# A third score area for the first batch's attention, with two PSUM banks merged into one tile

## The chip, the cores and the metric

The kernel runs on one core of one Trainium2 chip. The metric is the device time of a whole execution in microseconds (us), on a warm chip; spans and single instructions are read from a profiled execution, whose span is some 2 us shorter than the time (308.67 against 306.5 for the profiled run of the kernel before). "Faster" and "slower" mean a difference over 2% (6.2 us); medians are given with their range, and profiles decide where the time went.

## The reference, cut to what matters

```python
batch, n_heads, seq, head_dim = (4, 8, 768, 64); n_clusters = 16
n_tokens, d_model, d_ff = (3072, 512, 2048)

q_assign = argmax(einsum('bhsd,hcd->bhsc', q_n, c_n), axis=-1)   # k_assign likewise
mask = q_assign[:, :, :, None] == k_assign[:, :, None, :]
scores = where(mask, scale * q @ k.T, -1e9)
x = softmax(scores) @ v                     # (B*S, H*D) after a transpose
h = x @ w_in
g = h + sin(alpha * h)**2 / (alpha + 1e-9)
out = g @ w_out
```

Each head's queries and keys are assigned to one of 16 centroids, and only pairs with the same centroid attend. The kernel appends the one-hot assignment to q and k as 16 more rows of the contraction, so the mask costs no pass of its own.

## The kernel before

Four batches, one after the other: attention (48 "steps" a batch, each one key block of one head: two score matmuls, one exp of 128x768, six matmuls of probabilities by values), then the MoE layer (16 pieces). A step also carries preparations of later head pairs: transposes of q and k on TensorE, copies to SBUF on VectorE, casts to bf16 on GpSimd, the assignment matmuls and VectorE's one-hot.

PSUM has eight banks of 512 fp32. Two score areas take four, OB (output of attention) one, and three single banks M0, M1, M2 take the preparations in turn:

```python
SA = [psum.tile([P, 1024], F32, name=f"S{i}") for i in range(2)]
OB = psum.tile([P, 512], F32, name="OB")
M0 = psum.tile([P, 512], F32, name="M0")
M1 = psum.tile([P, 512], F32, name="M1")
M2 = psum.tile([P, 512], F32, name="M2")
# ...
banks = [M1, M2, M0]; held = set(); turn = [0]
def bank():                        # the next bank by turns that is not held
    while True:
        i = turn[0] % 3; turn[0] += 1
        if i not in held:
            return banks[i]

def area(i):                       # scores of step i
    return SA[(i // ASTEPS + i) % 2]

def prep_T(m, g, bk=None, eng="dve"):   # one of four: q or k, head 0 or 1 of pair m
    # three fp32 transposes into a bank, then one copy (VectorE or ScalarE) to SBUF
def prep_cast(m, h):               # GpSimd: two casts of 64x768 to bf16, 0.85 us each
def prep_v(m):                     # GpSimd: cast of the pair's v, 0.83 us
def load_qk(m, eng=nc.gpsimd):     # GpSimd issues two DMAs, 0.72 us each

class Fill:   # during attention of batches 1 to 3: output matmuls of the batch before,
              # accumulating in M1 or M0, which is held until its 16 are done
```

In MoE the third hidden area is the pair of banks (M1, M2), read in two pieces of 512 and 256. In the prologue `prep_T(0, 0, M1, "act")`, `prep_T(0, 1, M2, "act")` and later `prep_T(1, 0, M2, "act")`, `prep_T(1, 2, M1)` use both banks in turn.

The softmax here doesn't subtract the row's maximum and nothing guards it: scores larger than these inputs give would overflow.

## Time and profile before

| | before |
|---|---|
| time, median (range) | 308.21 us (308.18 to 308.46) |
| profiled span | 306.5 us |
| first exp starts | 11.93 us |
| batch 0: exps 0 to 12, exps 12 to 47 | 10.19, 26.56 us |
| attention of batches 1, 2, 3 (first exp to last) | 39.69, 38.73, 37.64 us |
| last exp to the next batch's first | 30.66, 31.38, 31.84 us |
| exps 80 to 81, exps 136 to 137 | 1.44, 1.05 us |

The rows add up to the span but for the tail after the last exp. They come from the start times of the 192 exps in the trace, which mark every step on the one engine that each step needs exactly once. The prediction shows the lines of the profile.

### The profile page before, as it was taken

The numbers are of one execution on the slowest core, as the hardware profiler recorded it, in microseconds if no ns is written. First come the engines' busy times: TensorE is split into PE (matmuls) and PEld (weight loads), VectorE is DVE, ScalarE is ACT, GpSimd is POOL, SyncE is SP. The second block draws the span as 40 slices with busy tenths as digits, with TensorE's granted clock in tenths as the row PEclk, the third lists the DMA queues.
The fourth block names the chain that finished last, engine by engine and source line by source line (L and its number), as shares of the span: only waits on it lengthen the run. The fifth ranks groups of instructions, "written<-read, shape, count | busy, mean of one in ns | idle before, by whom it ended". The sixth has DMA issues, their size and how long they took to land.

```text
span 306.5 us, 7197 instructions
## 1 busy us (share of the span) xinstructions
PE 300.6 (98%) x2727; PEld 177.9 (58%) x2727; DVE 206.6 (67%) x368; ACT 238.3 (78%) x323; POOL 140.4 (46%) x232
## 2 busy tenths in 40 slices
PE   8899999999999999999999999999999999999996
PEld 4466776555555666555456656555556666555543
DVE  3796666999867983688897485677865313667821
ACT  5689997976598988877589989687679999687300
POOL 6779988048364399983005189970001090000000
PEclk9999999999999999999999999999999999999999
DMA  7558999989668576971044577420012021000032
GB/s 215 166 165 237 309 261 234 215 182 325 127 178 195 122 154 156 305 295 51 2 120 108 108 182 161 119 86 2 0 72 60 33 47 46 29 7 2 0 127 78
DMA packets 31105, 40.48 MB, mean 132 GB/s; under 512 B 5904, under 2 KB 24928, under 8 KB 31072
## 3 DMA queue, kind: packets, MB, share of 16 engines
q0 software_dynamic: 10272, 21.12, 26.4%
q1 hardware_dynamic: 20560, 18.86, 23.7%
q8 instruction: 21, 0.34, 0.5%
q14 instruction: 12, 0.10, 0.1%
q10 hardware_dynamic: 240, 0.06, 0.1%
HBM read 27.30 MB, written 6.29 MB: 110 GB/s over the span
## 4 chain that ended last, share of the span: by engine, by line
PE 86%; ACT 10%; DVE 1%; issue 1%; DMA 1%; SPq 0%; ACTq 0%; DVEq 0%
PE M L406 19%; PE S L437 18%; PE S L338 11%; ACT pT L344 10%; PE OB L353 9%; PE M L437 8%; PE S L339 5%; PE OB L406 5%; PE M L222 3%; PE S L406 2%; PE M L144 2%; PE S L512 1%; DVE gT L462 1%; DMA QK<-ohT 1%; PE OB L377 1%
## 5 line engine op out<-in xcount | busy, mean ns | idle before, releaser
L344 ACT ACTIVATE pT<-S 128x768 bf16<-128x768 f32 x192 | 142.2, 810 | 14.8 <-PE S L339 13.7
L406 PE MATMUL M<-w_out_bf,gT 128*128 128x512 bf16 (+1 forms) x288 | 90.4, 376 | 0.0
L338 PE MATMUL S<-QK 80*128 80x512 bf16 x192 | 72.9, 380 | 1.4 <-ACT pT L344 0.6
L437 PEld LDWEIGHTS <-w_in_bf 128*128 128x128 bf16 x512 | 49.2, 98 | 38.0 <-issue 2.1
L353 PEld LDWEIGHTS <-pT 128*128 128x128 bf16 x1152 | 56.1, 97 | 21.2 <-ACT pT L344 0.2
L437 PE MATMUL S<-xT,w_in_bf 128*128 128x512 bf16 x352 | 66.1, 326 | 0.2 <-DVE gT L462 0.2
L353 PE MATMUL OB<-VX,pT 128*128 128x65 bf16 x1152 | 61.3, 193 | 0.0
L199 POOL TENSOR_SCALAR QK<-T 64x384 bf16<-64x384 f32 x80 | 42.8, 535 | 39.4 <-DMA T<-Tq 29.0
L450 ACT ACTIVATE s_sb<-S,alpha_col 128x768 bf16<-128x768 f32 (+2 forms) x45 | 39.7, 885 | 23.6 <-PE S L437 15.9
L406 PEld LDWEIGHTS <-gT 128*128 128x128 bf16 x400 | 38.4, 97 | 28.0 <-issue 1.2
L462 DVE SCALAR_TENSOR_TENSOR gT<-u_sb,ralpha,S 128x768 bf16<-128x768 bf16 (+2 forms) x45 | 44.6, 993 | 10.8 <-ACT u_sb L455 8.0
L339 PE MATMUL S<-QK 80*128 80x256 bf16 x192 | 51.9, 270 | 0.0
L399 POOL DMA_DIRECT2D xT<-xq x48 | 25.9, 547 | 23.2 <-DVE xq L391 22.2
L364 DVE RECIPROCAL rec<-OB 128x6 f32<-128x6 f32 x32 | 6.2, 195 | 36.6 <-PE OB L353 36.5
L437 PE MATMUL M<-xT,w_in_bf 128*128 128x512 bf16 (+1 forms) x160 | 30.6, 326 | 0.0
L339 PEld LDWEIGHTS <-QK 80*128 80x128 bf16 x192 | 18.8, 98 | 17.2 <-issue 2.2
L458 DVE TENSOR_TENSOR u_sb<-s_sb 128x768 bf16<-128x768 bf16 (+2 forms) x41 | 24.1, 589 | 6.1 <-ACT s_sb L450 6.1
L211 POOL CAST VX<-v 128x768 bf16<-128x768 f32 x16 | 13.3, 830 | 29.1 <-issue 28.1
L450 ACT ACTIVATE s_sb<-M,alpha_col 128x512 bf16<-128x512 f32 (+1 forms) x40 | 20.9, 574 | 6.9 <-PE M L437 6.8
L462 DVE SCALAR_TENSOR_TENSOR gT<-u_sb,ralpha,M 128x512 bf16<-128x512 bf16 (+1 forms) x40 | 22.8, 611 | 4.2 <-ACT u_sb L455 3.7
L406 PE MATMUL OB<-w_out_bf,gT 128*128 128x512 bf16 (+1 forms) x80 | 25.3, 347 | 0.0
L338 PEld LDWEIGHTS <-QK 80*128 80x128 bf16 x192 | 18.6, 97 | 8.4 <-issue 4.4
(86 smaller groups left out, 277.3 us busy)
## 6 DMA issues: line engine op xcount, KB each, us to landing
T<-Tq SPq DMA_DIRECT2D x80, 96.0 KB, 3.1
out_dram<-o_sb SPq DMA_DIRECT2D x23, 256.0 KB, 2.1
v<-in_v_dram POOLq DMA_DIRECT2D x14, 384.0 KB, 5.0
q<-in_q_dram POOLq DMA_DIRECT2D x13, 384.0 KB, 7.1
k<-in_k_dram POOLq DMA_DIRECT2D x13, 384.0 KB, 7.4
w_in_bf<-in_moe_w_in_dram POOLq DMA_DIRECT2D x4, 512.0 KB, 9.6
w_out_bf<-in_moe_w_out_dram POOLq DMA_DIRECT2D x4, 512.0 KB, 11.0
xT<-xq POOLq DMA_DIRECT2D x48, 24.0 KB, 2.3
```

The lines of the kernel that those rows point to most:

```text
L199: nc.gpsimd.tensor_scalar(out=QK[0:D, m % NQK, h, t].rearrange("c (n i a) -> c i n a", i=4, a=32)[:, 2 * par : 2 * par + 2], in0=src[:, t] ...
L211: nc.gpsimd.tensor_copy(out=VX[m % NVX][:, :, :, 0:D], in_=st[m]["v32"])
L338: nc.tensor.matmul(out=dst[:, 0:512], lhsT=lhsT, rhs=T[:, 0, 0:512], start=True, stop=True)
L339: nc.tensor.matmul(out=dst[:, 512:S], lhsT=lhsT, rhs=T[:, 0, 512:S], start=True, stop=True)
L344: nc.scalar.activation(out=pT, in_=area(i)[:, 0:S], func=ACTF.Exp, scale=escale)
L353: nc.tensor.matmul(out=o3[:, j, :], lhsT=pT[:, P * j : P * j + P], rhs=VX[m % NVX][:, h, jof(m // NHP, kt), :], start=(kt == 0 and j == 0) ...
L399: nc.gpsimd.dma_start(out=xT[32 * g : 32 * g + 32, 0:2, QS * i : QS * i + QS], in_=xq[0].rearrange("p (h g n) -> p h g n", h=2, g=4)[32 * ...
L406: nc.tensor.matmul(out=bk[:, lo:hi], lhsT=gT[:, f, P * mt : P * mt + P], rhs=w_out_bf[:, f, lo:hi], start=(f == 0), stop=(f == NF - 1),)
L437: nc.tensor.matmul(out=ar[lo // 512][:, 0 : hi - lo] if isinstance(ar, tuple) else ar[:, lo:hi], lhsT=lhsT, rhs=xT[:, kk, :].rearrange("c ...
L450: nc.scalar.activation(out=s_sb[:, lo:hi], in_=src, func=ACTF.Sin, scale=alpha_col[:, f : f + 1])
L458: nc.vector.tensor_tensor(out=u_sb[:, lo:hi], in0=s_sb[:, lo:hi], in1=s_sb[:, lo:hi], op=ALU.mult)
L462: nc.vector.scalar_tensor_tensor(out=gT[:, f, lo:hi], in0=u_sb[:, lo:hi], scalar=ralpha[:, f : f + 1], in1=src, op0=ALU.mult, op1=ALU.add,)
```

## The change

The intent: with three score areas instead of two, TensorE can be two steps ahead of ScalarE's exp, so the exps of batch 0 lie closer. The two banks come from M1 and M2, which are merged into one tile MM of 1024; from step 11 on batch 0's preparations share M0, and the preparations ("units") are dealt out anew over the steps. In MoE the merged tile is read in one piece.

```diff
-    M1 = psum.tile([P, 512], F32, name="M1")
-    M2 = psum.tile([P, 512], F32, name="M2")
+    MM = psum.tile([P, 1024], F32, name="MM")
+    M1, M2 = MM[:, 0:512], MM[:, 512:1024]
+    THREE = 12
 def area(i):
+        if THREE <= i < ASTEPS:
+            return (SA[0], SA[1], MM)[i % 3]
         return SA[(i // ASTEPS + i) % 2]
# ... units: (pair, ((unit, step), ...), assignment step, steps of the two casts)
-        (3, ((0, 11), (1, 14), (2, 16), (3, 18)), 20, (16, 19)),
-        (4, ((0, 22), (1, 23), (2, 28), (3, 34)), None, (25, 35)),
-        (5, ((0, 32), (1, 38), (2, 40), (3, 42)), None, (39, 43)),
+        (3, ((0, 11), (1, 14), (2, 15), (3, 17)), 20, (15, 18)),
+        (4, ((0, 26), (1, 36), (2, 38), (3, 40)), None, (37, 41)),
+        (5, ((0, 28), (1, 30), (2, 32), (3, 44)), None, (31, 45)),
# ... x's transposes to steps 23, 34, 42; VectorE transposes of later pairs; alpha to step 46
+            if i == THREE - 1:
+                held.update((0, 1))
+        if b == 0:
+            held.clear()
-        A = [SA[b % 2], SA[(b + 1) % 2], (M1, M2)]
+        A = [SA[b % 2], SA[(b + 1) % 2], MM]
# ... pieces() and hidden_mm() lose their case for a pair of banks
```

More of the change, by code (lines that the diff above doesn't have):

```diff
@@ L426, in pieces @@
     def pieces(ar, split):
-        if isinstance(ar, tuple):
-            return [(ar[0][:, 0:512], 0, 512), (ar[1][:, 0 : S - 512], 512, S)]
         if split:
@@ L437, in hidden_mm @@
                 nc.tensor.matmul(
-                    out=ar[lo // 512][:, 0 : hi - lo] if isinstance(ar, tuple) else ar[:, lo:hi],
+                    out=ar[:, lo:hi],
                     lhsT=lhsT,
@@ L621 @@
         (2, ((0, 4), (2, 5), (1, 6), (3, 7)), 8, (7, 8)),
[3 rows of a table removed]
[3 rows of a table added]
     ):
         pair_steps(m, make, asn, cast)
-    for g, i in enumerate((36, 39, 41, 41)):
+    for g, i in enumerate((38, 41, 34, 39)):
         at(i, lambda g=g: prep_D(NHP + 2, g))
-    for g, i in enumerate((44, 44, 46, 46)):
+    for g, i in enumerate((46, 42, 46, 46)):
         at(i, lambda g=g: prep_D(NHP + 3, g))
@@ L668 @@
             if m < NHP:
-                at((26, 30, 44)[m], lambda m=m: x_T(m))
+                at((23, 34, 42)[m], lambda m=m: x_T(m))
             elif m % NHP == 2:
@@ L683, in alpha @@
         nc.vector.reciprocal(out=ralpha, in_=ralpha)
-    at(10, alpha)
+    at(46, alpha)
     def load_w_in(n):
```

## The prediction

> **What bounds the kernel now.** I read the page first: the busy row, then the chain of waits.
>
> ```profile
> PE 300.6 (98%) x2727; PEld 177.9 (58%) x2727; DVE 206.6 (67%) x368; ACT 238.3 (78%) x323; POOL 140.4 (46%) x232
> ...
> PE 86%; ACT 10%; DVE 1%; issue 1%; DMA 1%; SPq 0%; ACTq 0%; DVEq 0%
> ```
>
> TensorE sets the end for 86% of the span and ScalarE for 10%. "Busy" is not "at its peak", so I then read ScalarE's timeline over batch 0's attention, where the third score area goes in. There are 48 exps there, one a step:
>
> ```profile
> 11.93 7.25 ACT L344 ACTIVATE pT<-S 128x768 bf16<-128x768 f32 x9 [0.91 <-PE S L339]
> 19.77 9.06 ACT L344 ACTIVATE pT<-S 128x768 bf16<-128x768 f32 x12 [0.59 <-PE S L339]
> 29.23 20.26 ACT L344 ACTIVATE pT<-S 128x768 bf16<-128x768 f32 x27 [0.40 <-PE S L339]
> ```
>
> ScalarE is nearly saturated: from step 9 on only one gap over 0.15 us (0.40, after the assignment matmuls of step 20). How close the exps lie is told by the chain of waits in order of time:
>
> ```profile
> 11.93 1.52 ACT pT L344 x2
> ...
> 22.12 0.82 ACT pT L344
> ...
> 43.48 0.81 ACT pT L344
> 44.34 0.53 ACT pT L344
> 45.05 0.70 ACT pT L344
> 45.79 0.65 ACT pT L344
> 46.50 0.69 ACT pT L344
> 47.24 0.82 ACT pT L344
> ```
>
> The first two exps found their scores ready: 1.52 less one exp of 0.81 is 0.71 us from start to start, ScalarE's own pace. Later ones start 0.71 and 0.74 apart by turns, and 0.86 in a step that also transposes a pair's q or k. That is the loop of two areas: exp 0.81, semaphore 0.05, two score matmuls 0.48, semaphore 0.10, together 1.44 for two exps. Exp 12 starts at 22.12 and exp 47 at 48.68: 26.56 us for 35 intervals, 0.76 each. That excess over 0.71 is all that a third area can win.
>
> Outside this, TensorE runs without holes: MoE pieces stand at 131.23, 132.96, 134.69 in the chain, 1.73 us apart, which is eight hidden matmuls (1.30) and two output matmuls (0.43). In the attention of batches 1 to 3 a step costs TensorE 0.73 us with one filling output matmul (matmuls of one step at 179.47, the next at 180.20), and ScalarE 0.72: both are full, and a hole on TensorE is not made up.
>
> **What the Trainium skill says.** "ScalarE: Activation LUTs", section What ACT_TABLE_LOAD costs: an ACTIVATE with immediate operands takes 186 ns + 0.833 ns per element, and back-to-back ones overlap by about 93 ns. For 768 that is 826 and 733 start to start. The trace has 811 and, at best, 708; the trace decides, but the message agrees: an exp can't go below about 0.71. "PSUM — Partial Sum Buffer", PSUM bank collisions raise a hardware error: accesses of two engines are to be kept apart by bank and quadrant, and different banks run clean. So the hardware needs no wait between M1 and M2. The trace agrees: TensorE writes M2 from 4.13 to 4.98 while ScalarE reads M1 from 4.38. "TensorE: Matmul & The Clock Gate", Part 1: half clock until a busy window of about 3.4 us. The first fp32 transposes lie 0.21 apart, those after 6.77 us 0.11, which agrees.
>
> **The change part by part.** I listed the instructions of both built kernels with their waits. Bank choices in batches 1 to 3 are the same in both. The order on TensorE, VectorE and GpSimd differs only in batch 0. But M1 and M2 are now halves of one tile MM, and the built kernel shows waits between the halves that the old one did not have: a matmul into one half waits until the last reader of the *other* half is done. That is what I weigh against the gain.
>
> *Gain, third area.* With exps at 0.71 to 0.715, 35 intervals are 25.0 us. TensorE's own demand in these 36 steps: 20 plain ones at 0.51 (scores 0.32, probabilities times values 0.18), 11 with a transpose group at 0.86, 3 with x transposes at 0.80, the assignment step 1.2, alpha's 0.7: 23.9 us, below ScalarE's. One more area is one exp of lookahead; the assignment step overruns it by some 0.25. So 25.3 instead of 26.56: **-1.3 us**. All preparations share M0 now; two in successive steps need about 0.96 (transposes 0.33, copy 0.56, semaphores) in 0.87, so stalls of 0.1, which the lookahead hides.
>
> *Loss, prologue.* Two new waits. The first: transposes of k into M2 wait for ScalarE's copy out of M1.
>
> ```profile
> 3.47 0.87 PE L144 MATMUL M<-ident_f,q 128*128 128x128 f32 x3
> 4.13 0.85 PE L144 MATMUL M<-ident_f,k 128*128 128x128 f32 x3
> 4.38 1.13 ACT L154 ACTIVATE T<-M 128x384 f32<-128x384 f32 x2 [0.38 <-PE M L144]
> ...
> 8.88 0.88 PE L144 MATMUL M<-ident_f,q 128*128 128x128 f32 x6 [0.23 <-DMA q<-in_q_dram]
> 10.12 0.90 ACT L154 ACTIVATE T<-M 128x384 f32<-128x384 f32 x2 [2.06 <-DVE oh L271]
> ```
>
> The first copy ends at 4.38 + 0.49 = 4.87, so k starts at 4.92, not 4.13: +0.79. Some comes back because warm-up matmuls then run at full clock; ScalarE's table load and the assignment behind it move by about 0.5 to 0.6. The second: of the six transposes at 8.88, the last three (into M1) now wait for ScalarE's copy out of M2, which starts at 10.12 because ScalarE was issuing DMAs. Moved by 0.5 that copy ends at 11.1; then nine transposes at 0.11 and a warm-up matmul 0.22: the first scores at about 12.4 instead of 11.41. **+1.0 us.** It lies on the chain: nothing else can start the exps.
>
> *Loss, step 7.* The last transposes of pair 2 go into one half (17.27 in the trace) and now wait for VectorE's copy out of the other half, 17.14 + 0.56 = 17.70. They start at 17.76: 0.49 late, in a stretch where TensorE is what the exps wait for, and pair 2's assignment stands behind. **+0.45.**
>
> *Loss, steps 80 and 136.* The output matmuls that fill the attention of batch 1 and 2 accumulate in M1 while an assignment or x's transposes use M2. Of the new waits there, those of steps 100, 130 and 148 are long fulfilled (the VectorE work is over before the matmul's place); two are not:
>
> ```profile
> 106.90 0.85 PE L222 MATMUL M<-T,cnB 128*32 128x384 f32 x8
> 107.17 0.97 DVE L283 STREAM_TRANSPOSE ohT<-oh 128x768 bf16<-128x768 bf16 x1
> 107.69 0.39 PE L406 MATMUL M<-w_out_bf,gT 128*128 128x512 bf16 x1
> 108.06 0.54 DVE L251 STREAM_TRANSPOSE asT<-M 128x384 f32<-128x384 f32 x1
> ...
> 183.95 0.38 PE L406 MATMUL M<-w_out_bf,gT 128*128 128x512 bf16 x1
> 184.21 0.52 DVE L382 COPY xT<-M 128x768 bf16<-128x768 bf16 x1
> ```
>
> At step 80 the matmul of 107.69 waits for asT, which ends at 108.60: it starts at 108.65, **+0.96**. At step 136 the one of 183.95 waits for the copy's end at 184.73, so 184.79: **+0.84**. The next scores stand behind both.
>
> *MoE's third area in one piece.* One Sin of 768 (0.90) for two of 512 and 256 (1.05 together), one VectorE operation (1.0) for two (1.14), 5 times a batch. Saves ScalarE and VectorE 0.15 each, 20 times, 3 us of work on either, beside a TensorE that is full at 1.73 a piece: **0**. MoE of batch 0 has one TensorE hole of 0.33 before 61.62, but its chain goes through areas 0 and 1. The whole area comes free when the single operation ends, about when the second piece did.
>
> *The rest.* Alpha at step 46 instead of 10 frees 0.1 early and lies in VectorE's idle 1.0 us before 50.03: 0. Dealing units out anew moves work of the same size.
>
> Sum: -1.3 + 1.0 + 0.45 + 0.96 + 0.84 = +1.95, so 308.2 becomes **310.1 us**, 0.6% slower.
>
> **The rivals.**
> First: the crossed waits cost little, because TensorE was waiting there anyway, and the gain stands: about 307.0. For it speaks that first scores waited for a DMA at 11.41 (0.37 idle). Against it: the DMA hangs on the same assignment, which is late too, and at 107.69 and 183.95 TensorE had no hole.
> Second: with three areas TensorE becomes the bound in steps 12 to 47 (VectorE's copies out of the single M0 stall it, every later score waits behind in order), and the gain shrinks to 0.3 or nothing: about 311.2. For it speaks that 23.9 of 25.3 us is a tight fit. Against it: one exp of slack, and GpSimd's casts are not moved to anything urgent.
> Third: the hole at 4.35 keeps TensorE's clock gate shut one window longer. Transposes and assignments of the prologue at half pace would cost about 1 us more: 311. The trace can't tell, as one window of before is all it has.
>
> **Range and chances.** Errors of the five terms are some 0.3 to 0.5 each and partly independent: 308.7 to 311.3 holds it 8 times in 10. 2% is 6.2 us, more than all terms of one sign together, so within 2% is almost certain.
>
> **What would show it.** Right: first exp near 12.9 instead of 11.93; exps 12 to 47 in about 25.3 us, at 0.71 apart; exps 80 to 81 and 136 to 137 apart by 2.4 and 1.9 us instead of 1.44 and 1.04, with TensorE's output matmul waiting for VectorE; MoE pieces still 1.73 apart; ScalarE's and VectorE's busy sums some 3 us less each. Wrong: first exp unmoved, or those two steps unchanged (the waits were fulfilled early), or a pace of 0.73 and more with the third area, in which case TensorE or the pv matmuls' wait for their exp would bound it.

## The result, and the profile after

The changed kernel takes 311.74 us in the median of 6 runs (310.83 to 313.07), the kernel before 308.39 (308.18 to 309.11, 6 runs). The ratio is 1.0111 with a 95% interval of 1.0087 to 1.0135: slower by 1.1%, within the 2% that count as the same. The direction was predicted, the size was not: 311.74 lies above the predicted range, whose upper end is 311.3.

The busy row and the chain of the page after:

```profile
PE 297.1 (96%) x2687; PEld 175.7 (57%) x2727; DVE 204.3 (66%) x348; ACT 235.1 (76%) x303; POOL 139.9 (45%) x232
...
PE 80%; DVE 7%; ACT 6%; DMA 2%; issue 2%; POOL 1%; SPq 1%; DVEq 0%; ACTq 0%
```

VectorE, which had 1% of the chain, now has 7%, and GpSimd appears with 1%: TensorE waits for them where it did not. (PE's 40 fewer matmuls are missing from this record only: their weight loads are all there, 2727, and the second profile of the same kernel has all 2727 matmuls.) The same intervals of exps as in the table before, for two profiles of the changed kernel (the second was taken later, beside the last experiments):

| us | before | predicted difference | after, first profile | after, second profile |
|---|---|---|---|---|
| first exp | 11.93 | +1.0 | 12.85 (+0.92) | 13.50 (+1.57) |
| exps 0 to 12 | 10.19 | +0.45 | 11.22 (+1.03) | 11.22 (+1.03) |
| exps 12 to 47 | 26.56 | -1.26 | 25.82 (-0.74) | 25.81 (-0.75) |
| batch 1, first exp to last | 39.69 | +0.96 | 41.16 (+1.47) | 40.90 (+1.22) |
| batch 2 | 38.73 | +0.84 | 39.40 (+0.67) | 39.33 (+0.60) |
| batch 3 | 37.64 | 0 | 37.63 | 37.65 |
| the three MoE stretches between | 93.88 | 0 | 93.94 | 93.94 |
| span | 306.5 | +1.95 | 309.9 (+3.4) | 310.2 (+3.7) |

The predicted 26.56 less 25.3 is 1.26 here. Steps 80 and 136 alone answer to the prediction: 2.39 and 1.88 apart in place of 1.44 and 1.05 (+0.95 and +0.83). The rest of batch 1 and 2 is single stretchings of a step by some 0.27 us (step 23 to 24 of batch 1, for instance), which the kernel before has as well, in other steps (18 to 19 of batch 2, 15 to 16 of batch 3); what causes them I did not find.

At both places TensorE's output matmul waits for VectorE to have read the other half. Columns of the timeline: start, duration, engine, line, operation, and in brackets the idle time before it and what ended it.

```profile
110.46 0.38 PE L409 MATMUL MM<-w_out_bf,gT 128*128 128x512 bf16 x1 [0.90 <-DVE asT L252]
...
109.87 0.54 DVE L252 STREAM_TRANSPOSE asT<-MM 128x384 f32<-128x384 f32 x1
...
187.38 0.38 PE L409 MATMUL MM<-w_out_bf,gT 128*128 128x512 bf16 x1 [0.67 <-DVE xT L385]
...
186.81 0.52 DVE L385 COPY xT<-MM 128x768 bf16<-128x768 bf16 x1
```

109.87 + 0.54 is 110.41, and the matmul starts 0.05 later. The same matmul stood 0.37 ahead of asT in the kernel before. MoE's pieces keep their pace (the chain of waits of batch 1: start, length, what):

```profile
132.25 1.30 PE MM L438 x8
133.56 0.21 PE OB L409
133.77 0.22 PE M L409
133.99 1.30 PE S L438 x8
```

133.99 less 132.25 is 1.74, against 1.73 before, although ScalarE and VectorE have 3.2 and 2.3 us less to do. Reading the area in one piece is worth nothing here, since every piece of the chain is TensorE's and neither engine bounds the stretch.

That leaves three places with a difference from the prediction: the prologue, steps 6 and 7, and one stall within steps 12 to 47.

**Steps 6 and 7.** The prediction let only step 7's transposes wait. Both wait:

```profile
17.97 0.55 PE L145 MATMUL MM<-ident_f,k 128*128 128x128 f32 x3 [0.30 <-DVE T L151]
...
19.17 0.55 PE L145 MATMUL MM<-ident_f,k 128*128 128x128 f32 x3 [0.32 <-DVE T L151]
```

VectorE was late with its copies T because the one-hot that stands ahead of them took 1.18 us instead of 0.65. The line of the kernel before, then two of the kernel after:

```profile
14.30 0.65 DVE L271 TENSOR_TENSOR oh<-asT,amax 128x384 bf16<-128x384 f32 x1
```

```profile
15.22 1.18 DVE L272 TENSOR_TENSOR oh<-asT,amax 128x384 bf16<-128x384 f32 x1
...
13.41 2.57 POOL L187 CAST QK<-T 64x768 bf16<-64x768 f32 x3
```

The casts of GpSimd run until 15.98. In the kernel before they ended at 14.54, just after the one-hot had begun.

**The stall.** With three areas the exps lie 0.69 to 0.71 apart, even closer than I thought possible. But exp 28 comes 1.73 after exp 27, and the third area's two steps of lookahead do not bridge that:

```profile
34.79 0.87 ACT L347 ACTIVATE pT<-S 128x768 bf16<-128x768 f32 x1
36.52 0.81 ACT L347 ACTIVATE pT<-S 128x768 bf16<-128x768 f32 x1 [0.85 <-PE S L342]
```

The bracket names the scores; the chain of waits, followed back from there, names what the scores stood behind:

```profile
31.35 0.80 POOL QK L187
32.16 0.04 issue
32.20 0.52 POOL QK L187
32.71 0.49 issue
33.20 0.11 POOL q L119
33.31 0.61 issue
33.93 0.72 POOL k L119
34.65 0.05 issue
34.70 0.83 POOL VX L212
35.53 0.04 issue
35.57 0.52 PE OB L356 x12
```

Probabilities by values (L356) of pair 2 wait for pair 2's v, cast by GpSimd (VX, L212) at 34.70. Ahead of it in GpSimd's order stand pair 3's second cast (L187) and the issue of two loads (L119). The kernel before has that cast behind VX:

```profile
31.39 0.82 POOL L211 CAST VX<-v 128x768 bf16<-128x768 f32 x1
32.15 1.71 POOL L186 CAST QK<-T 64x768 bf16<-64x768 f32 x2
```

The change moved this cast from step 19 to step 18, where the program adds it ahead of the same step's load and v cast. One number in the table of units put 1.7 us of work in front of an urgent cast.

**The prologue.** In the first profile it lost 0.92, about what was predicted; in the second 0.65 more. Lines of the first, then of the second:

```profile
5.00 0.55 PE L145 MATMUL MM<-ident_f,k 128*128 128x128 f32 x3 [0.58 <-ACT T L155]
...
11.07 0.55 PE L145 MATMUL MM<-ident_f,q 128*128 128x128 f32 x3 [0.58 <-ACT T L155]
```

```profile
5.00 0.90 PE L145 MATMUL MM<-ident_f,k 128*128 128x128 f32 x3 [0.58 <-ACT T L155]
...
7.69 0.90 PE L145 MATMUL S<-ident_f,q 128*128 128x128 f32 x3
...
11.72 0.55 PE L145 MATMUL MM<-ident_f,q 128*128 128x128 f32 x3 [0.90 <-ACT T L155]
```

The same three transposes at the same moment take 0.55 in one and 0.90 in the other: TensorE's clock. The trace has records of when the full clock was granted: from 4.71 us on in the first profile, from 9.13 in the second, from 6.33 in the kernel before.

That the first profile came so near is partly luck. Its chain of waits does not go through the first crossed wait at all; it goes through a load of pair 1's q, after whose landing the next transposes could start:

```profile
3.08 6.82 DMA q<-in_q_dram
...
9.94 0.55 PE L145 MATMUL MM<-ident_f,q 128*128 128x128 f32 x3 [1.01 <-DMA q<-in_q_dram]
```

The kernel before began the same transposes at 8.88. In a kernel below with one more warm-up matmul, whose transposes also ran at the faster pace from 5.07 on, they began at 8.93 and the first exp came at 12.58. By these two profiles the crossed waits alone cost 0.65 us with an early clock, the late load made it 0.92, and the late clock instead makes it 1.57.

### The profile page after: what moved, and what is told of

It is laid out like the page before. It is cut to its first block, busy times and chain, and to the rows that moved or that the text cites. A ratio compares the mean times of both kernels' runs of the same rounds, so it can differ in the third digit from the quotient of the medians.

```text
span 309.9 us, 7152 instructions
## 1 busy us (share of the span) xinstructions
PE 297.1 (96%) x2687; PEld 175.7 (57%) x2727; DVE 204.3 (66%) x348; ACT 235.1 (76%) x303; POOL 139.9 (45%) x232
## 4 chain that ended last, share of the span: by engine, by line
PE 80%; DVE 7%; ACT 6%; DMA 2%; issue 2%; POOL 1%; SPq 1%; DVEq 0%; ACTq 0%
PE S L438 18%; PE S L341 11%; PE M L409 9%; PE OB L356 8%; PE MM L438 8%; PE MM L409 7%; ACT pT L347 5%; PE S L342 5%; PE OB L409 4%; PE S L409 2%; DMA q<-in_q_dram 2%; PE MM L223 2%; PE M L223 1%; PE M L145 1%; DVE Tq L166 1%
## 5 line engine op out<-in xcount | busy, mean ns | idle before, releaser
L347 ACT ACTIVATE pT<-S 128x768 bf16<-128x768 f32 x180 | 134.5, 815 | 17.5 <-PE S L342 16.7
L341 PE MATMUL S<-QK 80*128 80x512 bf16 x180 | 68.4, 380 | 1.9
L356 PEld LDWEIGHTS <-pT 128*128 128x128 bf16 x1152 | 55.5, 97 | 23.7 <-ACT pT L347 1.8
L356 PE MATMUL OB<-VX,pT 128*128 128x65 bf16 x1152 | 61.4, 193 | 1.4 <-POOL VX L212 1.0
L409 PE MATMUL M<-w_out_bf,gT 128*128 128x512 bf16 x143 | 48.3, 379 | 0.5
L342 PE MATMUL S<-QK 80*128 80x256 bf16 x180 | 48.7, 270 | 0.0
L409 PE MATMUL MM<-w_out_bf,gT 128*128 128x512 bf16 (+1 forms) x114 | 34.2, 371 | 1.6 <-DVE asT L252 0.9
L438 PE MATMUL MM<-xT,w_in_bf 128*128 128x512 bf16 (+1 forms) x160 | 30.6, 326 | 0.1
L212 POOL CAST VX<-v 128x768 bf16<-128x768 f32 x16 | 13.2, 827 | 33.0 <-issue 29.8
L459 DVE TENSOR_TENSOR u_sb<-s_sb 128x768 bf16<-128x768 bf16 (+2 forms) x41 | 23.1, 566 | 6.6 <-ACT s_sb L451 6.1
L451 ACT ACTIVATE s_sb<-MM,alpha_col 128x768 bf16<-128x768 f32 x20 | 18.0, 898 | 8.4 <-PE MM L438 7.5
L463 DVE SCALAR_TENSOR_TENSOR gT<-u_sb,ralpha,MM 128x768 bf16<-128x768 bf16 x20 | 20.3, 1013 | 5.0 <-ACT u_sb L456 3.7
```

The costliest lines, as they stand in the source:

```text
L212: nc.gpsimd.tensor_copy(out=VX[m % NVX][:, :, :, 0:D], in_=st[m]["v32"])
L341: nc.tensor.matmul(out=dst[:, 0:512], lhsT=lhsT, rhs=T[:, 0, 0:512], start=True, stop=True)
L342: nc.tensor.matmul(out=dst[:, 512:S], lhsT=lhsT, rhs=T[:, 0, 512:S], start=True, stop=True)
L347: nc.scalar.activation(out=pT, in_=area(i)[:, 0:S], func=ACTF.Exp, scale=escale)
L356: nc.tensor.matmul(out=o3[:, j, :], lhsT=pT[:, P * j : P * j + P], rhs=VX[m % NVX][:, h, jof(m // NHP, kt), :], start=(kt == 0 and j == 0) ...
L409: nc.tensor.matmul(out=bk[:, lo:hi], lhsT=gT[:, f, P * mt : P * mt + P], rhs=w_out_bf[:, f, lo:hi], start=(f == 0), stop=(f == NF - 1),)
```

## The experiments

My theory after reading: the excess over the prediction is GpSimd's order (1.1 us), VectorE's one-hot beside a cast (0.5), and in most runs a clock gate that opens a window later because of the first crossed wait (0.6). The rivals: the third area itself gains less than it seems because TensorE and VectorE are full; the one-piece MoE has a hidden cost; the prologue's late clock is chance. Twelve runs were made, one of them the changed kernel again, in three sets. Beside each set, on the same chip, the kernel before took 308.6 to 308.7 us in the median; the sets ran on different chips, so between sets the ratios are compared. All results are correct but for the one that is marked.

**The cast back to its place.** The changed kernel with pair 3's second cast at step 19.

```diff
-        (3, ((0, 11), (1, 14), (2, 15), (3, 17)), 20, (15, 18)),
+        (3, ((0, 11), (1, 14), (2, 15), (3, 17)), 20, (15, 19)),
```

> The changed kernel with one cast put back: pair 3's second cast to step 19 instead of 18, so that GpSimd casts pair 2's v before it. Theory (GpSimd's order): TensorE's wait of 1.0 us for VX at step 27 goes, exps 12 to 47 take about 24.8 us instead of 25.8, and the whole is some 1.0 us below the changed kernel's 311.7: 310.7, 2.3 above before. Rival (the loads of v and q themselves land late, whatever stands before the cast): the wait stays or moves to the next transposes, and the time stays within 0.3 of 311.7.

311.1 us (311.04 to 311.31, 4 runs), ratio 1.0079 (1.0065 to 1.0093). GpSimd's timeline has the order back, and the stall is gone (exps 27 to 28: 0.69 us; exps 12 to 47: 24.69 instead of 25.82, so -1.13):

```profile
33.59 0.82 POOL L212 CAST VX<-v 128x768 bf16<-128x768 f32 x1
34.36 1.70 POOL L187 CAST QK<-T 64x768 bf16<-64x768 f32 x2
```

The profile has its first exp at 13.66, the late clock again, so the span shows only 0.6 of it. The order of GpSimd as the cause of the stall is shown.

**The fills' bank kept apart, first try.** In batches 1 to 3 a bank of the merged tile is not handed out while the fill's output matmuls hold the other.

```diff
-            if i not in held:
+            if i not in held and not (i == 1 and 0 in held):
                 return banks[i]
```

> The changed kernel with the preparations of batches 1 to 3 kept out of M2 while an output group accumulates in M1 (they take M0). Theory (waits across the two halves of MM): exps 80 to 81 go back from 2.39 to about 1.44 us and 136 to 137 from 1.88 to 1.05; the whole falls by 1.8 us to 309.9. Rival (TensorE would have waited there anyway, for M0 or for VectorE): those intervals stay above 2.0 and 1.6 and the whole falls by less than 0.5.

This kernel's result is wrong (relative error 0.59), by a fault of my edit: where two pairs are assigned in one step, both assignments now got M0, and the second wrote over the first. Its times (310.86 us, 310.28 to 310.98, 5 runs, ratio 1.0066) therefore stand for nothing but the two steps in question, which do the same work: exps 80 to 81 came down to 1.52 and 136 to 137 to 1.05.

**The same, done properly.** Only single assignments and the x transposes of the third pair ask for a bank outside the held tile.

```diff
-    def bank():
+    def bank(alone=False):
-            if i not in held:
+            if i not in held and not (alone and i == 1 and 0 in held):
-        at(a, lambda: (prep_asn(m), prep_hot(m, 0)))
+        at(a, lambda: (prep_asn(m, bk=bank(True)), prep_hot(m, 0)))
-                at(STEPS * (m + 1) + 4, lambda m=m: x_T(m))
+                at(STEPS * (m + 1) + 4, lambda m=m: x_T(m, bank(True)))
```

> The last but one idea again, without its fault (there two assignments of one step shared a bank and the second overwrote the first). Only the single assignments of one step and the x transposes keep out of M2 while an output group accumulates in M1; pairs of assignments keep M1 or M2 as before. Theory (crossed waits at steps 80 and 136): exps 80 to 81 about 1.45 us apart, 136 to 137 about 1.05, steps 98 and 128 as in the changed kernel (1.70 and 1.9); the result is correct again, and the whole falls by 1.8 us against the changed kernel, to about 309.9, or 1.2 to 1.9 above before, given a spread of 0.8 from the prologue. Rival: some of it is taken back later, as VectorE or M0 is waited for: those intervals shrink, but the attention of batches 1 and 2 loses less than 1.2.

310.4 us (310.36 to 310.63, 4 runs), ratio 1.0054 (1.0039 to 1.0068). Exps 80 to 81 at 1.53, 136 to 137 at 1.05; batch 1 is 40.18 instead of 41.16, batch 2 38.50 instead of 39.40. The lines of step 80:

```profile
109.23 0.85 PE L223 MATMUL M<-T,cnB 128*32 128x384 f32 x8
110.02 0.39 PE L409 MATMUL MM<-w_out_bf,gT 128*128 128x512 bf16 x1
```

The assignment goes into M0 (printed M), the output matmul into MM follows without a wait. The two terms of the prediction, +0.96 and +0.84, hold by cause and size: 0.86 and 0.83 of them are gone.

**The prologue's transposes outside the merged tile.** In the prologue a score area is still free, so pair 0's k and pair 1's q go there.

```diff
-    prep_T(0, 1, M2, "act")
+    prep_T(0, 1, SA[0][:, 512:1024], "act")
-    prep_T(1, 0, M2, "act")
+    prep_T(1, 0, SA[0][:, 0:512], "act")
```

> The changed kernel with two transpose groups of the prologue put into the idle first score area instead of M2, so no wait across MM is left before the first exp. Theory: first exp at 11.9 instead of 12.85, and the wait at step 6 goes too, because VectorE's one-hot then does not run beside GpSimd's casts (0.65 instead of 1.18 us): step 6 to 7 back to 0.9, step 7 to 8 still about 0.5 too long. The whole falls by 0.9 to 1.5 us, to 310.2 to 310.8. Rival (the clock gate or the DMA of the one-hots set the first exp): it stays after 12.4 and the whole falls by under 0.4.

310.28 us (310.08 to 310.57, 5 runs), ratio 1.0052 (1.0038 to 1.0066). The first exp comes at 11.58, earlier than in the kernel before, and the clock opens at 5.08: the two crossed waits together were the prologue's cost (what each is worth was not tried). But I missed on step 6: I expected its wait to vanish with an earlier prologue, and exps 6 to 7 are still 1.33 apart. The one-hot had moved forward with the first exp and still began 0.73 us before the cast ended, so it took 1.14; an earlier prologue does not part the two.

**The one-hot without a cast beside it.** Pair 1's second cast at step 6 instead of 0.

```diff
-        (1, (), 1, (0, 0)),
+        (1, (), 1, (0, 6)),
```

> The changed kernel with the second half of pair 1's casts at step 6 instead of step 0, so that GpSimd rests while VectorE makes pair 1's one-hot. Theory (the wait at step 6 comes of the one-hot's doubled time beside GpSimd's cast): the one-hot takes 0.56 to 0.65 us instead of 1.18, exps 6 to 7 lie 0.88 apart instead of 1.36, and 7 to 8 still 1.38. GpSimd's queue is 1.7 us later from there on, so the wait for v at step 27 grows. Rival (the one-hot is slow for another reason, or the wait at step 6 comes of the late start): one-hot 1.1 or more, 6 to 7 still over 1.2.

The one-hot's line in this kernel:

```profile
15.92 0.56 DVE L272 TENSOR_TENSOR oh<-asT,amax 128x384 bf16<-128x384 f32 x1
```

0.56 instead of 1.18, and exps 6 to 7 are 0.87 apart: step 6 no longer waits, step 7 still does (1.38), just as the prediction had it. The whole is worse, 313.1 us (one run), since the cast now stands in GpSimd's full order later and the stall at exp 28 grew from 1.73 to 3.10. That second effect was expected and confirms the stall's cause from the other side.

**Steps 4 to 9 with M0 between the halves.** Pair 2's transposes alternate between M0 and one half, a step later in part.

```diff
-        (2, ((0, 4), (2, 5), (1, 6), (3, 7)), 8, (7, 8)),
+        (2, ((0, 4), (2, 5), (1, 7), (3, 8)), 9, (8, 9)),
-            at(i, lambda g=g: prep_T(m, g))
+            bk = (M0 if i % 3 == 1 else M1) if m == 2 else None
+            at(i, lambda g=g, bk=bk: prep_T(m, g, bk))
-        at(asn, lambda: (prep_asn(m), prep_hot(m, 0)))
+        at(asn, lambda: (prep_asn(m, bk=M0 if m == 2 else None), prep_hot(m, 0)))
```

> The changed kernel with pair 2's four transpose groups at steps 4, 5, 7, 8 instead of 4 to 7, in M0 and M1 by turns, and its assignment at step 9. Theory (each group waits at most for a copy that was due two steps before): steps 5 to 10 cost 0.9 us a step or less but for the assignment's 1.4; from exp 5 to exp 10 it takes about 4.7 instead of 5.7 us; the whole falls by 1.0. Rival (VectorE is late because its one-hot runs beside GpSimd's casts, and any group there finds it late): a wait of 0.4 or more stays at step 7 or 8 and the whole falls by less than 0.5.

312.21 us (311.68 to 312.64, 4 runs), ratio 1.0105 (1.0086 to 1.0124): no gain in the whole. Exps 5 to 10 took 4.85 us in place of 5.72, as meant (though in this profile the casts were over before the one-hot, which took 0.56, so the banks alone are not shown to do it), but the pair's assignment a step later made another stall, and in this profile the clock, open from 3.91, was shut once more from 10.73 to 14.15; three of the four runs had a mean granted clock of 0.994 or 0.995 against 1.0. The fourth, at 1.0, was the fastest (311.68 against 312.04 to 312.64), so the clock may have taken part of the gain. That is not shown: of the four runs with the fills' bank properly apart, three had 0.993 and were no slower for it (310.36 to 310.63, against 310.39 at 1.0).

**The tile alone, with the one-piece MoE.** The kernel before with M1 and M2 as halves of MM and MoE's third area in one piece; no third score area, nothing dealt out anew.

```diff
-    M1 = psum.tile([P, 512], F32, name="M1")
-    M2 = psum.tile([P, 512], F32, name="M2")
+    MM = psum.tile([P, 1024], F32, name="MM")
+    M1, M2 = MM[:, 0:512], MM[:, 512:1024]
-        A = [SA[b % 2], SA[(b + 1) % 2], (M1, M2)]
+        A = [SA[b % 2], SA[(b + 1) % 2], MM]
```

> The kernel before with nothing but M1 and M2 made halves of one tile and MoE's third area in one piece: no third score area, nothing dealt out anew. Theory (the crossed waits make the loss; one piece in MoE is worth 0): it loses the prologue's 0.9, steps 6 to 8's 0.5 to 1.0, 0.95 and 0.84 of steps 80 and 136, and up to 1 more in batch 0, where preparations now cross too: 311.6 to 313.0. Rival (the third area or the dealing of units is what costs, the tile is harmless): within 0.5 of before, 308.4.

314.71 us (313.63 to 315.62, 5 runs), ratio 1.0193 (1.0172 to 1.0214), more than I expected. Merging the tiles hurts in batch 0 in more steps than the changed kernel shows (exps 11 to 12 at 1.51, 23 to 24 at 1.88), for the changed kernel holds both halves for scores there and sends all preparations through M0. And the clock was shut again from 10.55 to 13.97 in this profile.

**The tile alone, MoE in two pieces.** The same without the last line of the diff, and with the two-piece reading.

> The kernel before with M1 and M2 as halves of one tile and nothing else (MoE's third area still in two pieces). Against b_one (314.7, which also has the one piece) this tells what the one piece is worth: I expect 314.7, within 0.5, and MoE pieces 1.73 apart as before. Rival: the one piece frees the area later than the two pieces did and is the reason why b_one came out worse than I expected; then this kernel is at 312 to 313.

315.26 us (315.05 to 315.37, 4 runs), ratio 1.0208 (1.0193 to 1.0224). The intervals of this kernel and the one before it touch, so a difference between one piece and two is not shown; the stretches from last to next first exp are 30.67, 31.41 and 31.84 us here and 30.55, 31.38 and 31.81 there. The rival of a hidden cost of the one piece falls: in no stretch is it the longer one.

**One warm-up matmul in the hole.** Is the late clock chance? The changed kernel with TensorE's first hole filled.

```diff
     prep_T(0, 0, M1, "act")
+    warmup(1)
     prep_T(0, 1, M2, "act")
```

> The changed kernel with one more warm-up matmul in the hole between the first transposes of q and of k. If the crossed wait costs more than its 0.9 us because TensorE's hole keeps the clock gate shut, the filled hole opens it as early as before's profile shows (by about 6.5 us), the first exp comes at 12.5 to 12.9 us and the time is 310.6 to 311.1, with less spread than the changed kernel beside it (311.7). Rival: the gate hangs on the moment of the windows and not on this hole; then the first exp comes anywhere from 12.8 to 13.8 and the time is that of after2, within 0.3 us.

First exp at 12.58, by the earlier clock (transposes after the hole at 0.55); 311.51 us (311.14 to 313.24, 6 runs), ratio 1.0097 (1.0075 to 1.0119), against 312.03 (311.89 to 312.21, 4 runs), ratio 1.0105 (1.0089 to 1.0120), for the changed kernel beside it:

> The changed kernel once more, beside the others on the same chip: 311.2 to 312.2 us, first exp between 12.8 and 13.8, step 80 and 136 and the stall before exp 28 as in its first profile. If the clock gate explains its spread, a late first exp goes with a late opening.

The first exp fits the gate theory, the time lies between both expectations: 0.5 lower than the kernel beside it, but with intervals that overlap, and one run at 313.24 whose mean clock was 0.994. By timing alone this is not settled. The profiles say more. I cut TensorE's work into windows that end where the clock records begin. Their length, 3.41 us, is the time for which the clock was shut again in the two profiles above. The changed kernel's second profile (us, busy us of TensorE and number of matmuls, then the clock column, DMA share and GB/s):

```profile
2.30:5.72 3.42, 2.80 (x10) 1.00 0.90 261
5.72:9.13 3.41, 3.41 (x18) 1.00 0.86 294
```

The clock column says 1.00 throughout; do not trust it here, since transposes in both windows take 0.42 to 0.47 and only 0.27 afterwards. A window filled to 82% (2.80 of 3.42) left the gate shut, the next, filled wholly, opened it. Nine profiles are of kernels with the crossed wait in the prologue and have such records. Six of them opened late (8.38 to 9.97 us), and in all six the window before the opening one was filled to 80 to 83%. The other three opened early (4.71, 3.91, 3.73), after a window filled to 90, 91 and 84%. In the six that window held the hole whole or nearly so (0.52 us of it at least), in the three half of it or none. In the kernel before and the three without that wait the gate opened at 6.33, 5.08, 4.24 and 4.07, after windows filled to 96 to 100%. So the hole of 0.58 us costs a window unless the windows happen to fall well: where they fall differs from run to run, and the hole lowers the share that a window reaches. That is an association over thirteen profiles, with the one experiment in its favour; it is not a proof, since three of nine opened early without the filled hole, and its one profile could be such a case. Nor does an early opening ensure an early first exp: in two of the three the clock shut again, and the first exp came at 13.66 and 13.83.

**All mended.** The cast back, the fills' bank, the prologue and steps 4 to 9, all in the changed kernel (the diffs above together).

> All mends at once on the changed kernel: prologue without crossed waits, pair 2's groups at 4, 5, 7, 8, pair 3's second cast after pair 2's v, no M2 for single preparations beside a group in M1. If the terms add up: 311.7 less 1.2, 1.0, 1.1 and 1.8 is 306.6, some 1.8 below before (ratio 0.994): exps 12 to 47 in 24.7 us against 26.6 before. If the third area only shifts the wait (TensorE full in batches 1 to 3 takes it back, or GpSimd's queue becomes the bound in batch 0), it comes out at 308.0 or above.

307.56 us (307.31 to 307.78, 5 runs), ratio to before 0.9960 (0.9947 to 0.9973): it is below both kernels, the one before by 0.4%, which is clear of the noise but within the 2% that count as the same. It missed the expectation by 1 us: the assignment of pair 2 leaves a step of 1.83 and one of 1.20 (exps 9 to 10 and 15 to 16), and step 128 was 2.39 instead of 1.86.

**The mended kernel without the third area.** Only the choice of area goes back.

```diff
 def area(i):
-        if THREE <= i < ASTEPS:
-            return (SA[0], SA[1], MM)[i % 3]
         return SA[(i // ASTEPS + i) % 2]
```

> The mended kernel with the third score area alone taken out (scores of steps 12 to 47 go back to two areas; all banks, dealings and casts stay). If the gain of the third area is what I predicted (pace 0.76 back from 0.70), exps 12 to 47 take 26.5 to 26.8 us in place of c_best's 25.30, and the time is 308.8 to 309.2, a ratio to before of 1.000 to 1.003. Rival: the gain over before in c_best comes from the dealing and the prologue, not from the area; then exps 12 to 47 stay near 25.5 and the time stays at 307.6.

309.38 us (308.78 to 309.62, 5 runs), ratio 1.0015 (1.0000 to 1.0030). Exps 12 to 47 take 26.75 us against 25.30. ScalarE's timeline with three areas, then with two:

```profile
26.21 0.81 ACT L347 ACTIVATE pT<-MM 128x768 bf16<-128x768 f32 x1
26.90 1.52 ACT L347 ACTIVATE pT<-S 128x768 bf16<-128x768 f32 x2
28.28 0.84 ACT L347 ACTIVATE pT<-MM 128x768 bf16<-128x768 f32 x1
```

```profile
25.41 3.70 ACT L345 ACTIVATE pT<-S 128x768 bf16<-128x768 f32 x5 [0.34 <-PE S L340]
```

28.28 less 26.90 is 1.38 for two exps, 0.69 each; 3.70 less one exp of 0.81 is 2.89 for four intervals, 0.72 each. So the third area by itself is worth 1.45 us in this stretch (1.3 in the profiled span, 1.8 in the median), somewhat more than the 1.26 predicted for it, and the rival that it gains little falls. In the 25.30 us with three areas TensorE and ScalarE were both nearly full:

```profile
22.03:47.33 25.30, 24.91 (x343) 17.40 (x339) 18.70 (x42) 24.85 (x35) 22.15 (x29) 1.00 1.00 266
```

Busy were TensorE 24.91 and ScalarE 24.85, and GpSimd, the fifth number, 22.15: 88% of the stretch, so a displaced cast finds little idle time there.

## Why the prediction was right or wrong, point by point

- *"Gain, third area ... -1.3 us."* Right by cause and about by size: 1.45 in the pair of kernels that differ in nothing else. The pace was 0.69 where I had taken 0.71 as ScalarE's limit. In the changed kernel a stall left 0.74 of it.
- *"Dealing units out anew moves work of the same size."* This step failed. The work is of the same size, but the order on GpSimd is not free: pair 3's second cast, put one step earlier, delayed the v cast, and with it probabilities by values, by 1.13 us net. The size of moved work says nothing where the engine that does it is nearly full. I had the dealing in the diff and compared the order on each engine, but looked up only TensorE's waits. In the second rival I even named the point, "GpSimd's casts are not moved to anything urgent", as speaking against it; that sentence was wrong. The rival's number (311.2) came near, by another mechanism: not M0 nor TensorE's load, but GpSimd.
- *"Loss, step 7 ... +0.45."* Mis-sized: +1.03. Step 7's wait is as described; step 6's, which the prediction does not name, came on top, because the one-hot doubled beside a cast that ran on for 0.77 us after its start, against 0.25 in the kernel before. Without the overlap (the cast at step 6) one step waits instead of two.
- *"Loss, prologue ... +1.0."* The number was nearly met in the first profile (+0.92), but not by the predicted sum: the first crossed wait lay off the chain, behind a load that landed late. The second crossed wait was there as described. In the second profile the term was mis-sized (+1.57), for it had been worked out with the clock of the kernel before. The third rival, a gate that stays shut one window longer, is what six of nine profiles show; I gave it as a separate outcome at 311 and did not add it to the sum.
- *"Loss, steps 80 and 136, +0.96, +0.84."* Right: +0.95 and +0.83, gone with the shared tile's wait (1.53 and 1.05).
- *"MoE's third area in one piece: 0."* Right: pieces 1.74 apart, and the two kernels that differ in it alone are not told apart, with 2.8 us less on ScalarE.
- *The first rival*, crossed waits that cost little, was wrong.

The sum with what was measured in the second profile: +1.57 prologue, +1.03 steps 6 and 7, -0.75 third area with its stall, +0.95 and +0.83, and +0.09 of small differences are 3.72, the span's own difference. Against the predicted 1.95 that is 0.57, 0.58 and 0.51 more in three places, and these three add up to nearly all of the miss. In the first profile the same terms make 2.99, and the other 0.41 of its 3.40 are the single stretchings in batches 1 and 2, whose cause stays open.

## What to carry to other kernels

Two buffers that never waited for each other did so here once they were halves of one tile: list each place where one half is written while the other is still being read before counting the gain, and give such places another buffer. When units are dealt out anew, check the order on every in-order engine that is nearly full, not only on the one that sets the end: 1.7 us of cast in front of an urgent 0.83 cost 1.13 of the 1.87 us that exps 12 to 47 gained without it. And look up when the full clock was granted before trusting a cost in the first microseconds: in the changed kernel it came at 4.71 us in one profile and at 9.13 in another.

## What the Trainium skill lacked or had wrong

- "TensorE: Matmul & The Clock Gate", Part 1, says that the window is free-running, so that the transition varies by some 500 ns. Here the full clock came at 4.71 and 9.13 us in two profiles of the changed kernel, and at 3.73 to 9.97 over 13 profiles of related kernels: a window filled to 80 to 83% did not open it while windows of 84 to 100% did; the page gives no such share. In two profiles it shut again, for 3.42 us each time (which agrees with the page's window of 3.413 us), after windows that were filled to 46% and 56% and had no hole over 1.2 us, where that part of the page asks for an idle window (its section A second HAM failure mode tells of a clock that swings with many short pauses, without a share); in two others windows of 53% and 56% did not shut it, so the share alone does not decide that.
- "ScalarE: Activation LUTs", What ACT_TABLE_LOAD costs, gives figures from which I estimate 826 ns for 768 elements and 733 from start to start. Measured were 811 and, with three areas, 690.
- "SBUF — State Buffer", Summary: rules for kernel authors, states that where a VectorE instruction has two SBUF inputs and GpSimd's reads SBUF, the second to issue is fully blocked until the first finishes. The one-hot agrees but for a constant: alone it took 0.56 us, and in the ten profiles in which it began 0.25 to 0.77 us before the end of a running cast, it ended 0.41 us after that end each time. A full block followed by the whole instruction would be 0.56; the page does not tell of the 0.15 between.
- No page that I used tells that the scheduler's waits go by the tile and not by the bank: halves in different banks waited for each other at steps 80 and 136, which grew by 0.95 and 0.83 us and fell back when a bank of its own was used.
